# Strassen sevens that finish three of their sums inside PSUM, two products later in the queue

## The chip, the core and the metric

The kernel runs on one core of a Trainium2 chip. The metric is the device time of one execution in microseconds (us): 1163.27 us before the change, the median of three runs (1162.8 to 1163.62). Less is better.

## What is computed

Attention with pooled keys and values makes a matrix x of 2304 tokens by 512. A mixture of four experts follows, and then a gated block whose output is the result:

```python
p = domain_probs / (domain_probs.sum(-1, keepdims=True) + 1e-09)
for e in range(E):                                   # 4 experts
    h = np.maximum(x @ w1[e], 0.0)                   # 512 -> 1024
    out += p[:, e:e + 1] * (h @ w2[e])               # 1024 -> 512
...
a, b = out @ g_w1, out @ g_w2                        # 512 -> 1024 each
result = ((a * b) @ w3) @ w_out
```

Everything is float32. Each matrix product is made from three TensorE matmuls of rounded halves (`mm3`, line 169): high by low, low by high, high by high.

## The kernel before, in words

There are three stretches. Attention and expert 0 take the first 276 us. Then come experts 1 to 3, twelve **hidden batches** (`batch`, line 1176): one for each of four blocks of 576 tokens. At the end, from 882 us on, come eight **gated batches** (lines 1317 to 1430): the four blocks once for each half of the gate columns.

In both kinds of batch the first layer uses Strassen's scheme with seven products in place of eight. `seven(j, sink)` (line 947) handles one pair of 128-column blocks (for a hidden batch, two blocks of the expert's first layer; for a gated batch, one block of each gate), for one block of tokens in two halves of 288. A batch runs four sevens, j = 0 to 3, and then the second layer ("g2"), whose matmuls have 512 columns and which adds up over the four sevens' outputs.

A `product` (line 934) is six matmuls of 128x288 into a PSUM bank. `bank_r` (line 163) deals out the eight banks in turn, and each product of before takes a new one. In the order of the program a seven does this, where u, v and x are scratch tiles, c1 and c0 the two results and every line is one product:

```
x = copy(A11*B11)                  ScalarE (ACT), line 955
  then settle(): what the seven before left over, sink(0)
u = S2*T2 + x                      VectorE (DVE), lines 953, 957
v = S3*T3 + u                      DVE
c1[0] = A22*T4 + v                 DVE
c1[1] = S1*T1 + v; u = S1*T1 + u   DVE, twice; then sink(1)
c0[0] = A12*B21 + x                DVE
c0[1] = S4*B22 + u                 DVE; sink(0) is left for settle()
```

A `sink` passes a result on. The hidden one (line 1160) applies Relu on ACT to all 576 columns, splits the result into halves (ACT copies the high half, line 175; GpSimd, called POOL in the profile, subtracts for the low one, line 176) and copies an edge on POOL. The gated one (line 1308) does nothing for c1, and for c0 multiplies it by c1 on DVE (line 1311) and splits it; `settle()` follows each seven there at once.

The instructions of an engine run in the order of this program; waits between engines follow from the tiles that they read and write. So what stands early in the program on ACT or DVE is done before what stands later, whether or not the later one is ready. Beside the sevens the same engines do other work: `round_some` (weights of later stages, five DVE operations a step, called as `meanwhile` in sevens 1 and 3 of most hidden batches), `stream.split` (ACT and POOL), `weights_of` (line 746: sums and halves of the weights of one pair; ACT, DVE and POOL), `prepare_x` (line 892: sums of the next block of x, called as `next_x` after gated sevens 0 to 2) and `give` (results of the second layer). `fetch_operand` (line 811) brings the operands of the next batch in over the SP queue; the list `USED` (line 809) is their order, and `behind(i)` is the place in the last seven where fetch i is issued.

Of the kernel before, what the change touches and what calls it, by code (L numbers as in the profile page):

```python
# [17 lines left out]
def fused_kernel(  # L18
# [150 lines left out]
    def mm3(ps, lh, ll, rh, rl, first, last):  # L169
        nc.tensor.matmul(ps, lh, rl, start=first, stop=False)  # L170
        nc.tensor.matmul(ps, ll, rh, start=False, stop=False)  # L171
        nc.tensor.matmul(ps, lh, rh, start=False, stop=last)  # L172
# [154 lines left out]
    with tc.manual_schedule():  # L327
# [481 lines left out]
        USED = [B11, T2, T3, T4, T1, B21, B22]  # L809
# [124 lines left out]
        def product(j, a, b):  # L934
            wh, wl = wop_t[j]
            ps = bank_r("s1")[:, :HB]
            for kc in range(2):
                mm3(ps, pick(wh, a, kc), pick(wl, a, kc), operand(kc, 0, b), operand(kc, 1, b), kc == 0, kc == 1)
            return ps
# [7 lines left out]
        def seven(j, sink, meanwhile=None, behind=lambda n: None):  # L947

            x, u, v = (late["small"].tile([P, HB], F32, tag=t, name=t, bufs=1) for t in "xuv")
            c1, c0 = (late["small"].tile([P, 2, HB], F32, tag="c", name=t, bufs=3) for t in ("c1", "c0"))  # L950

            def add(to, one, two):
                nc.vector.tensor_tensor(to, one, two, op=ALU.add)  # L953

            nc.scalar.activation(x, product(j, A11, B11), AF.Copy)  # L955
            settle()
            add(u, product(j, S2, T2), x)
            if meanwhile:
                meanwhile()
            add(v, product(j, S3, T3), u)  # L960
            behind(0)
            add(c1[:, 0], product(j, A22, T4), v)
            behind(1)
            p5 = product(j, S1, T1)
            add(c1[:, 1], p5, v)
            add(u, p5, u)
            sink(1, c1, None)
            behind(2)
            add(c0[:, 0], product(j, A12, B21), x)
            behind(3)  # L970
            add(c0[:, 1], product(j, S4, B22), u)
            pending.append(lambda: sink(0, c0, c1))
# [184 lines left out]
        def hidden(j, b, **kw):  # L1157
            at = (0, P - S % P) if b % 2 else (S - S % P, 0)

            def sink(n, c, other):  # L1160
                fc = j + n * NJ
                t = z_t[fc]
                r = c.rearrange("p a s -> p (a s)")
                nc.scalar.activation(r, r, AF.Relu)  # L1164
                hi_lo(t[:, 0], t[:, 1], r, nc.gpsimd)
                nc.gpsimd.tensor_copy(edge_of(fc)[:, :, at[1]:at[1] + S % P], t[:, :, at[0]:at[0] + S % P])
# [138 lines left out]
        def gated_rows(j):  # L1305
            t = g_t[j]

            def sink(n, c, other):
                if n == 0:
                    r = c.rearrange("p a s -> p (a s)")  # L1310
                    nc.vector.tensor_tensor(r, r, other.rearrange("p a s -> p (a s)"), op=ALU.mult)  # L1311
                    hi_lo(t[:, 0], t[:, 1], r, nc.gpsimd)
            seven(j, sink)
# [3 lines left out]
        for half in range(2):  # L1317
            for n_b, b in enumerate(g_order):
# [11 lines left out]
                if b % 2 == 0:  # L1330
                    edge = late["small"].tile([P, NJ, 2, P], F32R, tag="part", name="edge")
                for j in range(NJ):
                    gated_rows(j)
                    settle()
# [4 lines left out]
                    if b % 2 == 0:  # L1339
                        nc.gpsimd.tensor_copy(edge[:, j, :, :S % P], g_t[j][:, :, S - S % P:])  # L1340
                    else:
                        nc.gpsimd.tensor_copy(edge[:, j, :, P - S % P:], g_t[j][:, :, :P - S % P])
                    if j < 3:
                        next_x(0, spare_slot, j)

# [116 lines left out]
```

## Time and profile before

| what | value |
|---|---|
| time, median of three runs | 1163.27 us |
| span of the profiled execution, first to last instruction | 1162.3 us |
| TensorE (PE) busy | 1150.7 us, 99% |
| weight loads (PEld) busy | 1042.2 us, 90% |
| DVE, POOL, ACT busy | 794.8, 484.9, 382.0 us |
| granted TensorE clock, mean | 1.000 |
| hidden batches 1 to 12 begin | 275.92 to 788.44 us |
| gated batches 1 to 8 begin | 882.04 to 1122.9 us |

The span is the time between the first and the last instruction of one profiled execution; the run's time includes what lies around it. PE's matmuls are pipelined, so their durations overlap: the distance between the starts of two matmuls tells the rate, not the duration of one.

### The profile page before, as it was taken

Reading aid. Unit: us, or ns where it says so; the run is one execution under the profiler, and the core shown is the slowest. Engines: PE = TensorE matmul, PEld = TensorE weight load, DVE = VectorE, ACT = ScalarE, POOL = GpSimd, SP = SyncE. Lnnn points to the kernel's source line nnn. Section 1 sums busy time; section 2 is a strip of 40 time slices with the busy share of each in tenths; the row PEclk is TensorE's granted clock in tenths of the full one; section 3 lists DMA queues with packets and bytes.
Section 4 is the critical chain, followed back from the end, with each engine's and each line's share of the span. In section 5 each row is a group of like instructions: output and inputs, shape, how many; then the busy total and the mean of one; then the engine's idle time right before and its main releaser. Section 6 shows DMA issues by size and latency. Waiting matters only on the chain.

```text
span 1162.3 us, 19412 instructions
## 1 busy us (share of the span) xinstructions
PE 1150.7 (99%) x6806; PEld 1042.2 (90%) x6806; DVE 794.8 (68%) x1624; ACT 382.0 (33%) x699; POOL 484.9 (42%) x563
## 2 busy tenths in 40 slices
PE   7999999999999999999999999999999999999998
PEld 6888898999898998998989989889889999999998
DVE  6867553476586878667678577778687777775454
ACT  4543433245241334421314414124352333231110
POOL 6965212256452647635436745255001222342111
PEclk9999999999999999999999999999999999999999
DMA  9866434554877654668583588686485542945651
GB/s 214 203 151 143 150 104 143 184 195 173 282 235 235 203 149 151 219 191 259 167 264 96 161 237 238 160 267 144 136 192 211 204 166 112 328 162 189 233 189 46
DMA packets 233217, 217.53 MB, mean 187 GB/s; under 512 B 92960, under 2 KB 185376, under 8 KB 233120
## 3 DMA queue, kind: packets, MB, share of 16 engines
q1 hardware_dynamic: 232832, 215.78, 60.4%
q8 instruction: 53, 0.87, 0.3%
q10 hardware_dynamic: 288, 0.52, 0.1%
q14 instruction: 44, 0.36, 0.1%
HBM read 144.41 MB, written 71.83 MB: 186 GB/s over the span
## 4 chain that ended last, share of the span: by engine, by line
PE 93%; DVE 2%; issue 1%; DMA 1%; ACT 1%; POOL 1%; SPq 0%; DVEq 0%; ACTq 0%; POOLq 0%
PE g L171 17%; PE g L172 17%; PE g L170 17%; PE s L170 13%; PE s L171 13%; PE s L172 13%; PE sc L500 1%; PE x_ps L554 1%; PE at_ps L539 1%; DMA plain<-in_k_dram 0%; DMA raw<-in_moe_w_dram 0%; DMA plain<-gate 0%; POOL plain L837 0%; POOL w2l L176 0%; PE vp_ps L448 0%
## 5 line engine op out<-in xcount | busy, mean ns | idle before, releaser
L176 POOL TENSOR_TENSOR round<-plain,round 128x576 fp32r<-128x576 f32 (+1 forms) x131 | 189.7, 1448 | 395.3 <-ACT round L175 324.3
L172 PE MATMUL s<-xo,wh 128*128 128x288 f32 x840 | 248.3, 296 | 0.0
L170 PE MATMUL s<-xo,wh 128*128 128x288 f32 x840 | 248.3, 296 | 0.0
L171 PE MATMUL s<-xo,wl 128*128 128x288 f32 x840 | 247.8, 295 | 0.0
L170 PE MATMUL g<-w2l,round 128*128 128x512 f32 x540 | 211.5, 392 | 0.0
L172 PE MATMUL g<-w2h,round 128*128 128x512 f32 x540 | 210.9, 391 | 0.0
L171 PE MATMUL g<-w2h,round 128*128 128x512 f32 x540 | 210.8, 390 | 0.1
L953 DVE TENSOR_TENSOR plain<-s,plain 128x288 f32<-128x288 f32 x320 | 138.2, 453 | 88.6 <-PE s L172 60.8
L170 PEld LDWEIGHTS s<-xo,wh 128*128 128x128 f32 x840 | 158.0, 188 | 0.7
L171 PEld LDWEIGHTS s<-xo,wl 128*128 128x128 f32 x840 | 157.7, 188 | 0.7
L172 PEld LDWEIGHTS s<-xo,wh 128*128 128x128 f32 x840 | 158.0, 188 | 0.0
L175 ACT ACTIVATE round<-plain 128x576 fp32r<-128x576 f32 (+1 forms) x135 | 90.9, 676 | 162.0 <-DVE plain L1311 158.9
L172 PEld LDWEIGHTS g<-w2h,round 128*128 128x128 f32 x540 | 101.4, 188 | 21.3
L170 PEld LDWEIGHTS g<-w2l,round 128*128 128x128 f32 x540 | 101.5, 188 | 20.5 <-issue 0.8
L171 PEld LDWEIGHTS g<-w2h,round 128*128 128x128 f32 x540 | 101.4, 188 | 20.1 <-DVE round L692 0.4
L955 ACT ACTIVATE plain<-s 128x288 f32<-128x288 f32 x80 | 32.2, 403 | 234.8 <-PE s L172 234.4
L1164 ACT ACTIVATE plain<-plain 128x576 f32<-128x576 f32 x96 | 65.5, 682 | 129.9 <-DVE plain L953 116.9
L288 POOL TENSOR_TENSOR x5l<-x5l 128x256 uint32<-128x256 uint32 x80 | 59.6, 745 | 101.1 <-DVE x5l L287 97.9
L953 DVE TENSOR_TENSOR plain<-s,pb 128x288 f32<-128x288 f32 x160 | 69.6, 456 | 25.7 <-PE s L172 15.2
L692 DVE SCALAR_TENSOR_TENSOR round<-g,round 128x384 fp32r<-128x384 f32 x48 | 26.6, 554 | 69.6 <-ACT round L691 69.4
L170 PE MATMUL g<-xl,round 128*128 128x384 f32 x192 | 66.6, 347 | 0.0
L172 PE MATMUL g<-xh,round 128*128 128x384 f32 x192 | 64.6, 337 | 0.0
(252 smaller groups left out, 2202.3 us busy)
## 6 DMA issues: line engine op xcount, KB each, us to landing
xo<-keptx SPq DMA_DIRECT2D x63, 576.0 KB
raw<-in_moe_w_dram SPq DMA_DIRECT2D x64, 256.0 KB
plain<-acc SPq DMA_DIRECT2D x40, 256.0 KB
keptx<-xo SPq DMA_DIRECT2D x16, 576.0 KB
x5h<-in_moe_w_dram SPq DMA_DIRECT2D x128, 64.0 KB
x5h<-in_moe_w_dram SPq DMA_DIRECT2D x32, 256.0 KB
kept<-xo SPq DMA_DIRECT2D x12, 576.0 KB
acc<-plain SPq DMA_DIRECT2D x26, 256.0 KB
```

The costliest lines, as they stand in the source:

```text
L170: nc.tensor.matmul(ps, lh, rl, start=first, stop=False)
L171: nc.tensor.matmul(ps, ll, rh, start=False, stop=False)
L172: nc.tensor.matmul(ps, lh, rh, start=False, stop=last)
L175: nc.scalar.activation(hi, src, AF.Copy)
L176: (lo_eng or nc.vector).tensor_tensor(lo, src, hi.bitcast(F32), op=ALU.subtract)
L288: nc.gpsimd.tensor_tensor(au, au, bu, op=ALU.add)
L500: nc.tensor.matmul(sc[off:off + n, (hp % 2) * W:(hp % 2 + 1) * W], qT[:, hp, off:off + n], kT_t[b][:, hp * W:(hp + 1) * W], start=True, st ...
L539: nc.tensor.transpose(pt[:NK, g * P:(g + 1) * P], e[:, half * G + g, :], ident)
L692: nc.vector.scalar_tensor_tensor(hl, ps, 0.0, hh.bitcast(F32), op0=ALU.max, op1=ALU.subtract)
L953: nc.vector.tensor_tensor(to, one, two, op=ALU.add)
L955: nc.scalar.activation(x, product(j, A11, B11), AF.Copy)
L1164: nc.scalar.activation(r, r, AF.Relu)
```

## The change

Three additions of each seven go into the matmuls. Where an addend already lies in a PSUM bank, the later product is accumulated onto it (its first matmul has `start=False`): A12*B21 onto the bank of A11*B11, A22*T4 onto the bank of S3*T3 after DVE has added u to that bank in place, and S4*B22 onto the bank of S1*T1 after DVE has added u there. v becomes a copy by ACT. A22*T4, S4*B22 and both sinks of a seven become `rest`, which `settle()` runs after the next seven's second product, or at the end of the batch. A seven takes four banks in place of seven. The sinks read what lies in banks themselves: the hidden one in two Relus of 288 columns, the gated one in two multiplications of 288 and a copy. In gated batches `settle()` moves to the end of the four sevens and the edge copies into the sink. The order of the fetches is changed to fit.

```diff
--- before.py
+++ after.py
@@ -166,10 +166,10 @@
         m = (ring[0] - 1) % 8
         return bank_p(name) if m < 4 else bank_q(m - 4, name)
 
-    def mm3(ps, lh, ll, rh, rl, first, last):
-        nc.tensor.matmul(ps, lh, rl, start=first, stop=False)
-        nc.tensor.matmul(ps, ll, rh, start=False, stop=False)
-        nc.tensor.matmul(ps, lh, rh, start=False, stop=last)
+    def mm3(ps, lh, ll, rh, rl, first, last, onto=False):
+        nc.tensor.matmul(ps, lh, rl, start=first, stop=False, skip_group_check=onto)
+        nc.tensor.matmul(ps, ll, rh, start=False, stop=False, skip_group_check=onto)
+        nc.tensor.matmul(ps, lh, rh, start=False, stop=last, skip_group_check=onto)
 
     def hi_lo(hi, lo, src, lo_eng=None):
         nc.scalar.activation(hi, src, AF.Copy)
@@ -806,7 +806,7 @@
             at = 2 * kc * XO // 4
             return late["xo"][:, at:at + 2 * XO // 4].bitcast(F32)
 
-        USED = [B11, T2, T3, T4, T1, B21, B22]
+        USED = [B11, T2, T3, T1, B21, T4, B22]
 
         def fetch_operand(b, n):
             m = USED[n]
@@ -931,11 +931,12 @@
         def pick(w, a, kc):
             return w[0][:, a, kc] if a < 6 else w[1][:, 0, kc]
 
-        def product(j, a, b):
+        def product(j, a, b, onto=None):
             wh, wl = wop_t[j]
-            ps = bank_r("s1")[:, :HB]
+            ps = bank_r("s1")[:, :HB] if onto is None else onto
             for kc in range(2):
-                mm3(ps, pick(wh, a, kc), pick(wl, a, kc), operand(kc, 0, b), operand(kc, 1, b), kc == 0, kc == 1)
+                mm3(ps, pick(wh, a, kc), pick(wl, a, kc), operand(kc, 0, b), operand(kc, 1, b),
+                    kc == 0 and onto is None, kc == 1, onto is not None)
             return ps
 
         pending = []
@@ -946,30 +947,37 @@
 
         def seven(j, sink, meanwhile=None, behind=lambda n: None):
 
-            x, u, v = (late["small"].tile([P, HB], F32, tag=t, name=t, bufs=1) for t in "xuv")
-            c1, c0 = (late["small"].tile([P, 2, HB], F32, tag="c", name=t, bufs=3) for t in ("c1", "c0"))
-
             def add(to, one, two):
                 nc.vector.tensor_tensor(to, one, two, op=ALU.add)
 
-            nc.scalar.activation(x, product(j, A11, B11), AF.Copy)
+            x, u, v = (late["small"].tile([P, HB], F32, tag=t, name=t, bufs=1) for t in "xuv")
+            p11 = product(j, A11, B11)
+            nc.scalar.activation(x, p11, AF.Copy)
+            p22 = product(j, S2, T2)
             settle()
-            add(u, product(j, S2, T2), x)
+            add(u, p22, x)
+            p21 = product(j, S3, T3)
+            add(p21, p21, u)
+            nc.scalar.activation(v, p21, AF.Copy)
+            p12 = product(j, S1, T1)
+            c1, c0 = (late["small"].tile([P, 2, HB], F32, tag="c", name=t, bufs=3) for t in ("c1", "c0"))
+            add(c1[:, 1], p12, v)
+            add(p12, p12, u)
             if meanwhile:
                 meanwhile()
-            add(v, product(j, S3, T3), u)
             behind(0)
-            add(c1[:, 0], product(j, A22, T4), v)
+            product(j, A12, B21, p11)
             behind(1)
-            p5 = product(j, S1, T1)
-            add(c1[:, 1], p5, v)
-            add(u, p5, u)
-            sink(1, c1, None)
-            behind(2)
-            add(c0[:, 0], product(j, A12, B21), x)
-            behind(3)
-            add(c0[:, 1], product(j, S4, B22), u)
-            pending.append(lambda: sink(0, c0, c1))
+
+            def rest():
+                product(j, A22, T4, p21)
+                behind(2)
+                sink(1, c1, (p21, None), None)
+                product(j, S4, B22, p12)
+                behind(3)
+                sink(0, c0, (p11, p12), c1)
+
+            pending.append(rest)
 
         dec = None
         late["wo"] = rounded(g_wout, "wo")
@@ -1157,11 +1165,12 @@
         def hidden(j, b, **kw):
             at = (0, P - S % P) if b % 2 else (S - S % P, 0)
 
-            def sink(n, c, other):
+            def sink(n, c, banks, *_):
                 fc = j + n * NJ
                 t = z_t[fc]
                 r = c.rearrange("p a s -> p (a s)")
-                nc.scalar.activation(r, r, AF.Relu)
+                for a, bank in enumerate(banks):
+                    nc.scalar.activation(c[:, a], c[:, a] if bank is None else bank, AF.Relu)
                 hi_lo(t[:, 0], t[:, 1], r, nc.gpsimd)
                 nc.gpsimd.tensor_copy(edge_of(fc)[:, :, at[1]:at[1] + S % P], t[:, :, at[0]:at[0] + S % P])
             seven(j, sink, **kw)
@@ -1302,14 +1311,18 @@
         third = [t.rearrange("p a s -> p (a s)").rearrange("p (n s) -> p n s", s=HB) for t in z_t[NJ:]]
         spare_slot = [(third[2 * n][:, :3], third[2 * n + 1]) for n in range(2)]
 
-        def gated_rows(j):
+        def gated_rows(j, at):
             t = g_t[j]
 
-            def sink(n, c, other):
+            def sink(n, c, banks, other):
                 if n == 0:
-                    r = c.rearrange("p a s -> p (a s)")
-                    nc.vector.tensor_tensor(r, r, other.rearrange("p a s -> p (a s)"), op=ALU.mult)
-                    hi_lo(t[:, 0], t[:, 1], r, nc.gpsimd)
+                    for a, bank in enumerate(banks):
+                        nc.vector.tensor_tensor(c[:, a], bank, other[:, a], op=ALU.mult)
+                    hi_lo(t[:, 0], t[:, 1], c.rearrange("p a s -> p (a s)"), nc.gpsimd)
+                    to, p0, s0 = at
+                    nc.gpsimd.tensor_copy(to[:, j, :, p0:p0 + S % P], t[:, :, s0:s0 + S % P])
+                else:
+                    nc.scalar.activation(c[:, 0], banks[0], AF.Copy)
             seven(j, sink)
 
         for kc in range(2):
@@ -1329,19 +1342,16 @@
 
                 if b % 2 == 0:
                     edge = late["small"].tile([P, NJ, 2, P], F32R, tag="part", name="edge")
+                at = (edge, P - S % P, 0) if b % 2 else (edge, 0, S - S % P)
                 for j in range(NJ):
-                    gated_rows(j)
-                    settle()
+                    gated_rows(j, at)
                     if half == 0 and n_b == 0 and j < 2:
                         for f in stores[:4]:
                             f()
                         del stores[:4]
-                    if b % 2 == 0:
-                        nc.gpsimd.tensor_copy(edge[:, j, :, :S % P], g_t[j][:, :, S - S % P:])
-                    else:
-                        nc.gpsimd.tensor_copy(edge[:, j, :, P - S % P:], g_t[j][:, :, :P - S % P])
                     if j < 3:
                         next_x(0, spare_slot, j)
+                settle()
 
                 lead_in = S % P if b % 2 else 0
                 tiles = []
```


## Rows read from the trace of the kernel before

**Rows 1.** The page, parts 1 and 2: busy time by engine; granted TensorE clock in slices

```profile
PE 1150.7 (99%) x6806; PEld 1042.2 (90%) x6806; DVE 794.8 (68%) x1624; ACT 382.0 (33%) x699; POOL 484.9 (42%) x563
...
PEclk9999999999999999999999999999999999999999
```

**Rows 2.** Waits of PE: waiter, releaser: us in total, times, longest us

```profile
PE kT_ps L428 <- POOL pb L420: 4.5, 7, 1.6
...
PE g L171 <- DVE round L176: 0.2, 1, 0.2
```

**Rows 3.** Groups of instructions with shapes kept apart: busy us, mean ns | idle before

```profile
L953 DVE TENSOR_TENSOR plain<-s,plain 128x288 f32<-128x288 f32 x320 | 138.2, 453 | 88.6 <-PE s L172 60.8 <-ACT plain L955 25.4 <-ACT plain L1164 1.6
...
L955 ACT ACTIVATE plain<-s 128x288 f32<-128x288 f32 x80 | 32.2, 403 | 234.8 <-PE s L172 234.4
...
L1164 ACT ACTIVATE plain<-plain 128x576 f32<-128x576 f32 x96 | 65.5, 682 | 129.9 <-DVE plain L953 116.9 <-DMA turned<-plain 9.1 <-DMA plain<-acc 3.8
```

**Rows 4.** Timeline of PE in the first batch's third and fourth seven: start us, us

```profile
287.09 0.30 PE L170 MATMUL s<-xo,wh 128*128 128x288 f32 x1
...
292.67 0.30 PE L170 MATMUL s<-xo,wh 128*128 128x288 f32 x1
...
293.08 0.31 PE L170 MATMUL s<-xo,wh 128*128 128x288 f32 x1
293.23 0.30 PE L171 MATMUL s<-xo,wl 128*128 128x288 f32 x1
```

**Rows 5.** Timeline of ACT beside them

```profile
288.88 0.69 ACT L175 ACTIVATE round<-plain 128x576 fp32r<-128x576 f32 x1
289.47 0.39 ACT L955 ACTIVATE plain<-s 128x288 f32<-128x288 f32 x1
289.76 0.67 ACT L1164 ACTIVATE plain<-plain 128x576 f32<-128x576 f32 x1
290.47 0.69 ACT L175 ACTIVATE round<-plain 128x576 fp32r<-128x576 f32 x1
...
293.70 0.41 ACT L955 ACTIVATE plain<-s 128x288 f32<-128x288 f32 x1 [0.33 <-PE s L172]
```

**Rows 6.** Timeline of DVE there: two additions back to back

```profile
291.05 0.82 DVE L953 TENSOR_TENSOR plain<-s,pb 128x288 f32<-128x288 f32 x2
```

**Rows 7.** Timeline of PE, its weight loads and DVE around one wait of PE

```profile
874.72 0.39 PE L170 MATMUL g<-round 128*128 128x512 f32 x1
...
874.81 0.42 DVE L176 TENSOR_TENSOR round<-raw,round 128x256 fp32r<-128x256 f32 x1
...
875.29 0.19 PEld L171 LDWEIGHTS g<-round 128*128 128x128 f32 x1 [0.61 <-DVE round L176]
...
875.39 0.19 PEld L172 LDWEIGHTS g<-round 128*128 128x128 f32 x1
```

**Rows 8.** Timeline of DVE and ACT in the first batch's second seven

```profile
282.90 0.97 DVE L761 TENSOR_TENSOR plain<-raw 128x256 f32<-128x256 f32 x1 [0.74 <-DMA acc<-plain]
...
285.75 0.39 ACT L955 ACTIVATE plain<-s 128x288 f32<-128x288 f32 x1
```

**Rows 9.** Timeline of PE and DVE in the last batch of the third pass

```profile
788.44 0.29 PE L170 MATMUL s<-xo,wh 128*128 128x288 f32 x1
...
793.61 0.42 DVE L953 TENSOR_TENSOR plain<-s,plain 128x288 f32<-128x288 f32 x1
```

**Rows 10.** Timeline of DVE, PE and ACT between the two passes over the gates

```profile
1007.51 0.76 DVE L1311 TENSOR_TENSOR plain<-plain 128x576 f32<-128x576 f32 x1
1008.19 0.42 DVE L761 TENSOR_TENSOR x5h<-raw 128x256 f32<-128x256 f32 x1
...
1020.44 0.29 PE L170 MATMUL s<-round,wh 128*128 128x288 f32 x1
...
1025.86 0.40 ACT L955 ACTIVATE plain<-s 128x288 f32<-128x288 f32 x1
```

**Rows 11.** Timeline of DVE in the first gated batch: the longest preparation of x

```profile
890.22 1.68 DVE L902 TENSOR_TENSOR x5h<-plain,x5h 128x288 f32<-128x288 f32 x1
```

## Prediction

> **What bounds the kernel.** I read the page's busy times first: TensorE (PE) is busy for 1150.7 of 1162.3 us, at the full granted clock (2.4 GHz) in every slice, while DVE, POOL and ACT stand at 68%, 42% and 33% [rows 1]. Busy matmuls overlap, so this alone doesn't say that PE lacks nothing. The waits of PE are therefore next: of its six kinds the costliest is 4.5 us in all, in attention, and the last is 0.2 us; the wait of a seven for a bank, an operand or an addition is not among them [rows 2]. Third, the timeline of PE: sevens 2 and 3 of the first batch start 5.58 us apart [rows 4], so a product takes 5.58 / 7 = 0.80 us and a matmul 0.133 us. PE is thus the bound, and DVE's additions lie beside it. They can run late without harm: a product takes the next of eight banks, and PE may be some seven products (5.6 us) ahead before it needs a bank back.
>
> **What is removed and added.** There are 20 x 4 = 80 sevens. DVE drops from 7 additions to 4 in each, 240 x 0.453 = 109 us of its busy time [rows 3]. PE's matmuls are the same in number and shape; only the flag of the first one of three products differs, and matmuls with and without that flag are in the row of before at the same rate (the 5.58 us hold both). ACT gains the copy of v, 80 x 0.403 = 32 us, and in each of 96 hidden sinks two Relus of 288 for one of 576, 2 x 0.403 - 0.682 = 0.12 us, 12 us [rows 3]. The gated multiplication in two halves and the copy of c1[0] cost DVE and ACT about an operation more for each of 32 sevens. All this lies on engines with room, under PE's 5.58 us a seven, so it costs nothing where PE need not wait. The POOL copies of the edges are the same ones, issued right behind the same halves, with POOL at 42%. The fetches are as many; each waits on SP for its operand's last product, which for B11 to T1 comes early in the last seven, and for B21, T4 and B22 before the second layer begins. They have that layer to land, and no queue behind them feeds a seven; I cost them at nothing.
>
> **What is new** are waits of PE. In the order of the change A12*B21 may start only when ACT has copied x, A22*T4 when DVE has added u and ACT has copied v, S4*B22 when DVE has added u to S1*T1. PE's queue is in order, so whatever comes next waits too. A bank comes back after eight products or so, as before. The pattern is A11*B11, S2*T2, then A22*T4 and S4*B22 of the seven before, S3*T3, S1*T1, A12*B21. With another seven behind it, v is needed 5 products (4.0 us) after S3*T3 has begun; at the end of a batch the next seven's two and its waiting are missing, and it is 3 products (2.4 us). The cost is where this distance is short, and where ACT or DVE is late already.
>
> **The end of each hidden batch.** Let T be the start of rest(2), two products after the last seven began. PE's own order is A22*T4(2) at T, S4*B22(2) 0.80, S3*T3(3) 1.60, S1*T1(3) 2.39, A12*B21(3) 3.19, A22*T4(3) 3.99. ACT has to do both sinks of seven 2 before v(3). A product's result is in use 1.03 us after its start (292.67 to 293.70) [rows 4, 5]. An ACT operation of 288 lets an independent one begin after 0.29, one of 576 after 0.59, and one that needs it begins 0.03 after its end [rows 5]. So: Relu of c1[0] at T+1.03, of c1[1] 1.32, high half 1.77, Relu 2.36, Relu 2.65, high half 3.09, v at 3.68 until 4.08. DVE's addition to S3*T3 (ready at 2.63 + 0.46 = 3.09) is not the late one. A wait of PE costs the release and a weight load that could not run ahead: 0.06 and 0.10 in the one row that shows it, from the end of DVE's 874.81 + 0.42 to 875.29, and to the next weight load at 875.39 [rows 7]. A22*T4(3) thus starts at 4.24 in place of 3.99, +0.25. DVE's two further additions start at 4.12 and, 0.36 later [rows 6], at 4.48, until 4.94; with 0.16 that is 5.10 against 4.24 + 0.80, another 0.06. Together 0.31 a batch, 12 times: **3.7 us**. Bounds: the release alone and no weight load lost, 0.10, or 1.2 us in all; every ACT operation at its full length (seven of 0.403 or 0.69 and a gap each, v until 4.60) and the second addition behind its first, 0.95, or 11.4 us. An addition written into PSUM isn't in the trace; I take the 0.453 us of one that reads PSUM, and the upper bound has room for 0.1 us more.
>
> **Three places where an engine is late.** First batch, seven 1: ACT's x waits there for `weights_of`, whose sums on DVE start at 282.90 behind a DMA; x runs at 285.75 to 286.14 [rows 8]. In the new order A12*B21(1) would start 11 products after 275.92 (seven 2's 287.09 less two sevens), at 284.69, and gets 286.14 + 0.16: 1.61 late. ACT then still owes seven 0's sinks before v(1): 286.04 and the chain of above to v's end at 289.11, 289.27 against 288.69, 0.58, and 0.06 as above: **2.2 us** (1.5 to 2.6). Last batch of pass three: DVE's queue of weights and second-layer results leaves the first u at 793.61 until 794.03 [rows 9]; addition, v on ACT and release make 795.11 where A22*T4(0) is due 7 products after 788.44, at 794.02: **1.1 us** (0.5 to 1.3). Between the passes over the gates `weights_of` holds DVE and ACT, so that x of the next batch's first seven comes at 1025.86, 5.4 us after its product began [rows 10]. A12*B21(0) is due at 1020.44 + 3.19 = 1023.63 and would wait until 1025.86 + 0.40 + 0.16 = 1026.42, 2.8 us. DVE's chain of weights begins there 0.7 us sooner, since one multiplication of 0.46 replaces an addition and one of 0.76; if all of this reaches x it is 2.0. I take the middle, **2.4 us** (0 if the chain clears by itself, to 2.9).
>
> **Gated batches.** Before v(3) ACT has a copy and one high half only: multiplications at T+1.83, u at 2.20, addition 2.69, v at 3.19 until 3.59, additions at 3.62 and 3.98 until 4.44. Against 3.99 and 4.79, less 0.16 each, this leaves 0.24 and 0.19 us. x's preparation, with a longest operation of 1.68 us on DVE [rows 11], is issued behind the four additions and has until the next seven's multiplications. So **0**, and 0.4 for each of eight (3.2 us) as upper bound.
>
> **Sum.** 3.7 + 2.2 + 1.1 + 2.4 = 9.4 us. The span of 1162.3 us becomes 1171.7; the runs' median lies 1.0 us above the span, which I leave: **1172.7 us**. The bounds add up to 3.2 (1166.5) and 21.4 us (1184.7).
>
> **Against the change** speaks that three of a seven's four banks now stay open while other engines read and write them. By rows 4 to 6 the products between hide this, but for the last seven of a batch. If nothing hid it, each seven would show an addition, the copy of v and two additions, 0.46 + 0.40 + 0.36 + 0.46 = 1.7 us, and 80 of them 134 us; this is rival 5. The Trainium skill, "Perfetto Trace Analysis", section "Matmuls", has a rule on this side: independent groups of matmuls should go round different PSUM banks, so that emptying one overlaps the next group's matmuls.
>
> **Rivals.** (1) *The waits are covered*, and the time is that of before, 1163.3 us, not slower. Its place is ACT's order: if v(3) ends by T+3.83 in place of 4.08, and with 240 additions gone the late x and u come before 1023.5, 284.5 and 794, PE never waits. For it: DVE's 109 us; against: x is late there by `weights_of` and DMA, not by additions. 11%. (2) *ACT's chain is longer*, no overlap of its operations or dearer PSUM access: 11.4 us for 3.7, and up to 3.2 in the gated batches, 1180 to 1184 us. For it: the chain has seven operations in a row; against: rows 5 show the overlap. 17%. (3) *Faster*: PE's matmuls are up to 0.15 us apart in places (293.08 to 293.23) [rows 4], against a mean of 0.133; if engines reading PSUM cause that and the change relieves them by 0.1 us a seven, 8 us go, 1155 us. Against: reads of PSUM become more, not fewer. 5%. (4) *The clock*: after its first instruction PE stood still for at most 1.6 us at a time (longest wait of the first row) [rows 2] and kept its full clock [rows 1]; a stop of 2.4 us is new. Were the clock to fall to 1.2 GHz for one batch's four sevens, 22.3 us would be added, 1195 us. 3%. The Trainium skill, "TensorE: Matmul & The Clock Gate", section "What's actually happening", has an idle engine fall back to that level; no row of this trace shows it. (5) *Open banks stop PE in every seven*: 1163.3 + 134 = 1297 us. Against: DVE and ACT need 1.7 us of the 4.0 us that they have. 1%.
>
> **How the numbers follow.** My forecast, waits at batch ends and the three late places, gets 63%: 1166.5 to 1178 us. About 0.2% (2.3 us) is what a measurement of this kernel can tell from no change. Forecast, it and rivals 2, 4 and 5 are slower by more than that, 84%; rival 1 is the same, 11%; rival 3 is faster, 5%. The range takes part of rival 1 and most of rival 2 in: 1164 to 1181 us.
>
> **What would show it.** Waits of PE, or gaps between matmuls, for ACT's copies and DVE's additions at s: one of some 0.3 us before the last product but one of each hidden batch's sevens, three larger ones near 286, 795 and 1024 us. Within the sevens 0.80 us a product, as before. If the batches' sevens still take 22.3 us each, rival 1 or 3 holds; if the gaps stand in every seven, rival 5 does; if they stand at the ends but at 0.6 us and more, rival 2.

## The result, and the profile after

The change makes the kernel slower: 1173.05 us, the median of four runs (1171.64 to 1173.96), against 1163.12 us of before (also four). The ratio is 1.0083, its 95% interval 1.0069 to 1.0097. The span of the profiled execution, the slowest of the four, is 1172.2 us, 9.9 us more than before. The page's busy times, which answer to [rows 1]:

```profile
PE 1156.9 (99%) x6806; PEld 1043.5 (89%) x6806; DVE 692.0 (59%) x1416; ACT 432.1 (37%) x907; POOL 477.9 (41%) x563
```

DVE has lost 103 us of work and ACT has gained 50, and nothing of the 103 has come off the span. That is what PE at 99% meant in [rows 1]: DVE's work lay beside PE's. The groups with shapes kept apart (busy us, mean ns, idle before), as in [rows 3], say what the new operations cost:

```profile
L951 DVE TENSOR_TENSOR s<-s,plain 128x288 f32<-128x288 f32 x160 | 73.7, 461 | 58.3 <-PE s L172 54.7 <-DVE plain L951 0.5
...
L961 ACT ACTIVATE pb<-s 128x288 f32<-128x288 f32 x80 | 32.2, 403 | 42.9 <-DVE s L951 42.9
```

The addition in place, PSUM to PSUM, takes 461 ns, 8 ns more than one from PSUM to SBUF; the copy of v takes the 403 ns of the copy of x. So no new operation is dear. What is new are waits. Of the views of PE's waits (waiter, releaser: us in all, times, longest), first that of the matmuls, as in [rows 2]:

```profile
PE s L170 <- ACT plain L955: 3.0, 2, 2.3
...
PE s L170 <- ACT pb L961: 0.6, 2, 0.3
```

and that of the weight loads, which go ahead of the matmuls and so meet most waits first:

```profile
PEld s L170 <- ACT pb L961: 4.8, 14, 0.6
PEld s L170 <- ACT plain L955: 3.5, 2, 2.5
```

L961 is the copy of v, awaited 14 times (12 batch ends and two late places); L955 is the copy of x, awaited twice. The length of each batch's four sevens, from its first matmul's start to the start of the matmul that follows its last one, shows where the 9.9 us are:

| batches | before, us | after, us | difference, us |
|---|---|---|---|
| ten hidden ones | 22.34 each | 22.69 each | 10 x 0.35 = 3.5 |
| first hidden one (275.20) | 22.34 | 24.47 | 2.13 |
| last of pass three (793.63) | 22.34 | 23.40 | 1.06 |
| first of the second gate pass (1026.51) | 22.40 | 26.26 | 3.86 |
| seven other gated ones | 22.28 to 22.35 | 22.28 to 22.33 | 0.0 |
| all twenty | 446.72 | 457.29 | 10.6 |

The span grew by 0.7 less, since the first batch begins at 275.20, not at 275.92. That is scatter: in the profiles of the change, A, B, B2, F and G, whose programs are the same up to there, it begins between 274.32 and 276.33. Within the sevens the rate is nearly what it was (0.132 us a matmul, 0.133 before).

The end of a hidden batch, in the second one, as PE, ACT and DVE show it in the timeline (start us, us). T, the start of A22\*T4 of the third seven, is 338.14:

```profile
338.14 0.29 PE L170 MATMUL s<-xo,wh 128*128 128x288 f32 x1
...
339.20 0.41 ACT L1173 ACTIVATE plain<-s 128x288 f32<-128x288 f32 x1 [1.23 <-PE s L172]
...
339.51 0.44 ACT L1173 ACTIVATE plain<-plain 128x288 f32<-128x288 f32 x1
...
339.98 0.69 ACT L175 ACTIVATE round<-plain 128x576 fp32r<-128x576 f32 x1
...
340.57 0.69 ACT L1173 ACTIVATE plain<-s 128x288 f32<-128x288 f32 x2
...
341.29 0.69 ACT L175 ACTIVATE round<-plain 128x576 fp32r<-128x576 f32 x1
...
341.88 0.39 ACT L961 ACTIVATE pb<-s 128x288 f32<-128x288 f32 x1
341.96 0.29 PE L172 MATMUL s<-xo,wh 128*128 128x288 f32 x1
342.33 0.19 PEld L170 LDWEIGHTS s<-xo,wh 128*128 128x128 f32 x1 [0.31 <-ACT pb L961]
342.33 0.40 PE L170 MATMUL s<-xo,wh 128*128 128x288 f32 x1
...
342.57 0.30 PE L171 MATMUL s<-xo,wl 128*128 128x288 f32 x1
...
342.74 0.46 DVE L951 TENSOR_TENSOR s<-s,plain 128x288 f32<-128x288 f32 x1
```

ACT runs seven operations without a pause, v last, and v ends at 342.27. PE's matmul starts 0.06 us later, at 342.33, where it was due at 342.09; the matmul behind it comes after 0.24 us in place of 0.13, since its weights (342.44 in the trace) could not be loaded ahead. DVE's second addition ends at 343.20 and S4\*B22 starts at 343.25, 0.02 late, and again 0.24 passes behind its first matmul.

The dearest place is the stop between the two passes over the gates. PE's timeline there (with the wait that it shows), and ACT's copy of x:

```profile
1029.58 0.29 PE L172 MATMUL s<-xo,wh 128*128 128x288 f32 x1
...
1031.68 0.40 ACT L955 ACTIVATE plain<-s 128x288 f32<-128x288 f32 x1
...
1032.13 0.61 PE L170 MATMUL s<-round,wh 128*128 128x288 f32 x1 [2.26 <-ACT plain L955]
1032.54 0.44 PE L171 MATMUL s<-round,wl 128*128 128x288 f32 x1
1032.78 0.44 PE L172 MATMUL s<-round,wh 128*128 128x288 f32 x1
```

After the stop the matmuls come 0.24 us apart, until 1035.2. The view by windows (length, busy us of PE, PEld, DVE, ACT, POOL, then granted clock, DMA share, GB/s) has the reason:

```profile
1026.00:1029.50 3.50, 3.50 (x26) 3.38 (x26) 3.47 (x5) 2.99 (x7) 2.53 (x2) 1.00 0.54 203
1029.50:1032.00 2.50, 0.38 (x3) 0.14 (x2) 1.88 (x4) 1.85 (x4) 1.27 (x2) 0.96 0.16 61
1032.00:1035.20 3.20, 3.07 (x13) 3.07 (x14) 1.75 (x4) 0.49 (x2) 1.75 (x2) 0.50 0.84 235
1035.20:1040.00 4.80, 4.80 (x38) 4.80 (x38) 1.92 (x5) 1.92 (x4) 0.94 (x1) 1.00 0.82 330
```

The granted clock is 0.50 for these 3.2 us, which is 1.2 GHz, and PE looks busy there (3.07 of 3.20) while it does half the work.

### The profile page after: what moved, and what is told of

It reads as the page before. It is cut to its first block, busy times and chain, and to the rows that moved or that the text cites. A ratio compares the mean times of both kernels' runs of the same rounds, so it can differ in the third digit from the quotient of the medians.

```text
span 1172.2 us, 19164 instructions
## 1 busy us (share of the span) xinstructions
PE 1156.9 (99%) x6806; PEld 1043.5 (89%) x6806; DVE 692.0 (59%) x1416; ACT 432.1 (37%) x907; POOL 477.9 (41%) x563
## 4 chain that ended last, share of the span: by engine, by line
PE 87%; ACT 5%; DVE 3%; DMA 2%; issue 2%; POOL 1%; SPq 0%; ACTq 0%; DVEq 0%; POOLq 0%
PE g L171 16%; PE g L172 16%; PE g L170 16%; PE s L170 12%; PE s L172 11%; PE s L171 11%; ACT round L175 2%; ACT plain L1173 1%; PE sc L500 1%; PE at_ps L539 1%; PE x_ps L554 1%; DMA raw<-in_moe_w_dram 1%; DMA x5h<-in_moe_w_dram 0%; DMA plain<-in_k_dram 0%; ACT pb L961 0%
## 5 line engine op out<-in xcount | busy, mean ns | idle before, releaser
L955 ACT ACTIVATE plain<-s 128x288 f32<-128x288 f32 x80 | 32.9, 411 | 296.9 <-PE s L172 296.8
L951 DVE TENSOR_TENSOR s<-s,plain 128x288 f32<-128x288 f32 x160 | 73.7, 461 | 58.3 <-PE s L172 54.7
L951 DVE TENSOR_TENSOR plain<-s,pb 128x288 f32<-128x288 f32 x80 | 36.6, 457 | 68.8 <-ACT pb L961 63.7
L1173 ACT ACTIVATE plain<-s 128x288 f32<-128x288 f32 x144 | 53.0, 402 | 57.1 <-PE s L172 53.7
L951 DVE TENSOR_TENSOR plain<-s,plain 128x288 f32<-128x288 f32 x80 | 36.2, 453 | 61.2 <-PE s L172 55.5
```

Of the source, the lines that this page charges most:

```text
L955: nc.scalar.activation(x, p11, AF.Copy)
L1173: nc.scalar.activation(c[:, a], c[:, a] if bank is None else bank, AF.Relu)
```

## The experiments

The theory was: accumulating is free for PE; the late places of two products are free too; the loss is in short waits where A22\*T4, S4\*B22 and A12\*B21 now depend on ACT's and DVE's copies and additions. Its rivals: the late places or the changed fetches cost the time (D decides); accumulating onto a bank that others have read and written is slow by itself (A and E); waits of other kinds. Runs A, B, D and F share one chip and runs of before with a median of 1163.74 us (14 runs); the others share one with 1163.94 us (15 runs).

### D: the late places alone

No product accumulates; DVE makes all seven additions again, and the two products, the sinks and the fetches stay in their new places.

```diff
-            add(p21, p21, u)
-            nc.scalar.activation(v, p21, AF.Copy)
+            add(v, p21, u)
...
-            product(j, A12, B21, p11)
+            add(c0[:, 0], product(j, A12, B21), x)
...
-                product(j, A22, T4, p21)
+                add(c1[:, 0], product(j, A22, T4), v)
...
```

> No accumulation: seven banks a seven and all additions on DVE as before the change, but A22*T4, S4*B22 and the sinks stay in their late places (after the next seven's second product). Theory 1: the late places alone cost nothing, since no product waits for DVE or ACT but by the bank it takes, eight products back: 1162.5 to 1164 us, each hidden batch's sevens 22.3 us long without gaps. Rival (the late products are the cost, as they end later and hold the second layer up): 1167 us and more.

Measured: 1162.42 us (1161.88 to 1163.14, ten runs), ratio 0.9989 (0.9979 to 0.9998). All sevens take 22.21 to 22.26 us a batch without a gap, but for the batch at 786.99 with 23.22; there the sevens wait twice (spacings of 0.40 and 0.69 us), for results of `give` (line 1243). The view of PE's waits has one of the two:

```profile
PE s L170 <- DVE pb L1243: 0.4, 1, 0.4
```

The late places and the new order of fetches thus cost nothing; the whole loss belongs to the accumulations and what feeds them.

### E: the accumulations in the old places

The other half alone: A22\*T4, S4\*B22 and A12\*B21 accumulate as in the change, but stand where the kernel before had them, within their own seven.

```diff
             add(p21, p21, u)
             nc.scalar.activation(v, p21, AF.Copy)
...
+            product(j, A22, T4, p21)
+            p12 = product(j, S1, T1)
...
+            sink(1, c1, (p21, None), None)
+            product(j, A12, B21, p11)
+            product(j, S4, B22, p12)
             def rest():
-                product(j, A22, T4, p21)
...
                 sink(0, c0, (p11, p12), c1)
```

> The accumulations without the late places: A22*T4 directly behind S3*T3, S4*B22 two products behind S1*T1, as the products stood before the change; the sink of c1 at once. Theory 1: each seven now shows what the late places hide: A22*T4 waits for the addition and the copy of v, 1.3 us, S4*B22 for DVE's two additions, 0.4 us: 80 x 1.7 = 135 us more, less what the late x and u cost the changed kernel (it is hidden in these waits): 1290 to 1310 us. If accumulating itself were the cost and not the waits, the place would not matter: 1173 us.

Measured: 1316.62 us (two runs), ratio 1.1309 (1.1288 to 1.133), a little above what was expected. The waits of the weight loads are now there in every one of the 80 sevens:

```profile
PEld s L170 <- ACT pb L961: 106.7, 80, 4.8
PEld s L170 <- DVE s L951: 37.7, 78, 0.8
```

The timeline of PE has a matmul that waited for the copy of v and one that waited for an addition in place, each with the matmul before it:

```profile
402.01 0.29 PE L172 MATMUL s<-xo,wh 128*128 128x288 f32 x1
403.30 0.40 PE L170 MATMUL s<-xo,wh 128*128 128x288 f32 x1 [1.00 <-ACT pb L961]
...
405.65 0.29 PE L172 MATMUL s<-xo,wh 128*128 128x288 f32 x1
406.18 0.40 PE L170 MATMUL s<-xo,wx 128*128 128x288 f32 x1 [0.23 <-DVE s L951]
```

Before A22\*T4 1.3 us pass between matmuls, before S4\*B22 some 0.5, and 0.24 behind each, where 0.13 is the rate: 1.17 + 0.37 + 2 x 0.11 = 1.76 us a seven. That is the price that the late places hide: 80 x 1.76 = 141 us of the 152.7 lost, and most of the rest stands at the three late places. So the two halves of the change belong together: one costs nothing and the other is ruinous without it.

### A: the copy of v on DVE

```diff
-            nc.scalar.activation(v, p21, AF.Copy)
+            nc.vector.tensor_copy(v, p21)
```

> v is copied out of the bank by DVE, right behind the addition, and no longer by ACT behind both sinks of the seven before; all else as in the changed kernel (1173.05 us). Theory 1 (the waits at the end of hidden batches are for ACT's queue): v ends at about T+3.55 in place of T+4.1, so the gaps before the last two products of the twelve hidden batches (0.35 us a batch net, 4.2 us) go, and of the first batch's second wait about 0.5 us; the wait of 3.9 us between the passes over the gates stays: 1168 to 1169 us. Theory 2 (accumulating onto a bank that another engine has written is itself dear for TensorE): the gaps stay, 1172.5 to 1174 us.

Measured: 1167.9 us (1166.79 to 1168.72, five runs), ratio 1.0033 (1.002 to 1.0046). The timeline of the second batch has v and ACT's high half side by side, where ACT did one after the other:

```profile
339.99 0.46 DVE L961 COPY pb<-s 128x288 f32<-128x288 f32 x1
340.07 0.69 ACT L175 ACTIVATE round<-plain 128x576 fp32r<-128x576 f32 x1
```

The hidden batches, except the first and the last, take 22.22 us without a gap, though three products of each seven still accumulate onto banks that DVE has written. So accumulating is free for PE, and the end of a hidden batch costs what ACT's queue makes it cost. The gated batches gain nothing (22.32 to 22.37 us): there the spacing behind S4\*B22's first matmul is 0.24 us, as DVE's second addition, now behind the copy, ends only 0.06 us before that matmul. The three late places stay: 23.33 us for the first batch (it keeps the wait for x and loses that for v), 23.46 for the last of pass three, 24.94 for the stop between the gate passes.

### F: v copied twice on ACT

The copy of v is issued twice in a row on ACT, to see whether its time reaches PE.

```diff
             nc.scalar.activation(v, p21, AF.Copy)
+            nc.scalar.activation(v, p21, AF.Copy)
```

> The suspected cost doubled: ACT copies v twice in a row, so v is final about 0.30 us later and nothing else changes. Theory 1: every hidden batch's end waits 0.30 us longer, 3.6 us; the gated ends, where I worked out 0.2 us of slack, wait some 0.1 us longer, 0.7 us; the places where ACT is late (first batch, last batch of pass three) 0.3 us each: 1177 to 1178.5 us, and no gap elsewhere, since 1.4 us and more are free there. Theory 2 (ACT's queue is not what ends the waits): 1173 us.

Measured: 1182.76 us (1182.2 to 1183.45, four runs), ratio 1.0162 (1.0147 to 1.0177): the right places, but dearer than expected. The timeline at the end of the second batch:

```profile
342.02 0.39 ACT L961 ACTIVATE pb<-s 128x288 f32<-128x288 f32 x1
342.44 0.41 ACT L962 ACTIVATE pb<-s 128x288 f32<-128x288 f32 x1
...
342.90 0.40 PE L170 MATMUL s<-xo,wh 128*128 128x288 f32 x1 [0.52 <-ACT pb L962]
```

The second copy starts 0.42 us after the first, not 0.3, as it writes the same tile. So each hidden batch grows by 0.43 us (22.69 to 23.12), and most gated ones by 0.44 (22.32 to 22.75), where v's slack is used up and A22\*T4 comes some 0.3 us late, with the lost weight load behind it. The three late places grow too (25.50, 24.65 and 26.83 us). Within all other sevens there is no gap, so ACT's time counts only where the distance is short.

### B and B2: A12\*B21 in a bank of its own

A12\*B21 goes to a bank of its own and DVE adds x, so that PE no longer waits for x. In B the addition stands where the product was, behind the rounding step (`meanwhile`):

```diff
             if meanwhile:
                 meanwhile()
             behind(0)
-            product(j, A12, B21, p11)
+            add(c0[:, 0], product(j, A12, B21), x)
...
-                sink(0, c0, (p11, p12), c1)
+                sink(0, c0, (None, p12), c1)
```

> A12*B21 goes into a bank of its own again and DVE adds x (one of the three accumulations undone; the other two and the late places stay). Theory 1: the long wait between the passes over the gates is A12*B21 waiting for ACT's late x; it moves to A22*T4 of the same seven, which is due 2.4 us later, and shrinks from 2.4 to about 1.6 us; with the shorter stop TensorE's clock should not fall, which gives back another 1.2 us. In the first batch the wait only moves from A12*B21 to A22*T4. Ends of batches unchanged. 1170.5 to 1171.5 us. Theory 2 (accumulating itself is dear): a third of it goes, wherever the accumulations stand, some 3 us spread over all batches, 1170 us, with smaller gaps at batch ends.

Measured: 1179.85 us (1178.75 to 1181.34, four runs), ratio 1.0136 (1.0118 to 1.0154): a miss by 8 us. The place it was made for did what was expected (the batch after the gate passes takes 24.05 us with a stop of 1.69). But most hidden batches with rounding steps take 23.3 to 23.9 us, with gaps of 0.2 to 0.4 us before A22\*T4(2) and 0.7 before A22\*T4(3). DVE and ACT in the timeline of the second batch show why:

```profile
334.35 0.29 DVE L287 TENSOR_SCALAR x5l<-x5h 128x256 f32<-128x256 uint32 x1
334.56 0.45 DVE L951 TENSOR_TENSOR plain<-s,plain 128x288 f32<-128x288 f32 x1
335.10 0.41 ACT L955 ACTIVATE plain<-s 128x288 f32<-128x288 f32 x1 [3.51 <-DVE plain L951]
335.41 0.41 ACT L1173 ACTIVATE plain<-s 128x288 f32<-128x288 f32 x1
```

x is one tile. The new addition reads x(1) only behind the five operations of the rounding step (L282 to L287), so ACT can't write x(2) before 335.10, and the sinks and v, which stand behind x(2) in ACT's queue, are late with it. B2 tests that reading: the product and its addition are put ahead of the rounding step.

```diff
+            add(c0[:, 0], product(j, A12, B21), x)
             if meanwhile:
                 meanwhile()
             behind(0)
-            add(c0[:, 0], product(j, A12, B21), x)
```

> As the kernel with A12*B21 in a bank of its own, but this product and its addition of x stand ahead of the rounding step on DVE and not behind it. My reading of that kernel's 1179.9 us: x is one scratch tile, the addition of x behind the rounding step of sevens 1 and 3 keeps the next seven's copy of x from starting, and this copy is first in ACT's queue, ahead of both sinks and of v. If so, the gaps in sevens 2 and the 0.7 us gaps at batch ends fall back to none and 0.4 us, and the time is what I had expected there: 1170.5 to 1171.8 us. If the bank of its own (or the fifth bank a seven takes) is the cause: 1179 us and more.

Measured: 1172.34 us (1171.1 to 1176.03, four runs), ratio 1.0074 (1.0056 to 1.0092), half a microsecond above the upper end of what was expected. The batches are as they should be: 22.72 us for the hidden ones, no gap before A22\*T4(2), 24.08 for the one after the gate passes. The same two operations, in B2's timeline:

```profile
333.28 0.45 DVE L951 TENSOR_TENSOR plain<-s,plain 128x288 f32<-128x288 f32 x1
...
333.82 0.41 ACT L955 ACTIVATE plain<-s 128x288 f32<-128x288 f32 x1 [1.31 <-DVE plain L951]
```

B2's second batch begins at 322.72 and B's at 321.81, so counted from there the addition comes 2.19 us sooner (10.56 us after the batch began, not 12.75) and x(2) with it. So B's loss was its place in DVE's queue. Its ratio is still not far from the change's 1.0083: the stop between the gate passes is the only place that gains (2.2 us), while the ends of the hidden batches (0.38 us each) and the first batch (24.61 us) stay as dear.

### G: useless products in the long stop

Three products S1\*T1, 18 matmuls, go into a bank that nobody reads, ahead of A12\*B21 in the first seven after the gate passes. They take the time of the stop and do no useful work; if the low clock follows from the stop, it should vanish.

```diff
+            for _ in range(fill):
+                product(j, S1, T1)
             product(j, A12, B21, p11)
...
-                    gated_rows(j, at)
+                    gated_rows(j, at, 3 if half == 1 and n_b == 0 and j == 0 else 0)
```

> In the first seven after the change of gates (the one where TensorE stands still for 2.4 us) three copies of the product S1*T1 (18 matmuls, 2.4 us) are issued ahead of A12*B21 into a bank that nobody reads: TensorE works on something useless where it waited. Theory 1a (after the stop the granted clock is 0.50, and 12 or more matmuls start 0.24 in place of 0.133 us apart): A12*B21 begins at the same time, but at full clock; 1.2 to 1.5 us go wherever the changed kernel's run had a clock under 1.000: 1171.5 to 1172 us in every run, mean clock 1.000. Rival (the slow matmuls after the stop are slow because of what the other engines and the transfers do then): the 0.24 us spacing stays, 1173 us.

Measured: 1172.6 us (1171.59 to 1172.97, five runs), ratio 1.007 (1.0057 to 1.0082). The windows that showed the stop and the low clock in the change's profile:

```profile
1029.50:1032.00 2.50, 2.50 (x21) 2.50 (x20) 2.35 (x5) 1.39 (x3) 1.25 (x2) 1.00 0.36 135
1032.00:1035.20 3.20, 3.20 (x25) 3.08 (x24) 1.76 (x4) 1.36 (x4) 2.24 (x2) 1.00 0.62 179
```

The clock is 1.00 throughout, the matmuls are 0.13 us apart right behind the place of the stop (but for one 0.24), and the batch takes 24.83 us, 1.4 less than 26.26. That the filled stop is what kept the clock up is not shown: A's kernel has the same stop unfilled, its one profile has a clock of 1.00 behind it too (rows in the last section), and its batch takes 24.94 us. What A and G show is the size: some 1.3 of the 1.4 us are the clock's, and 0.1 is the weight load lost behind a wait, which A's batch pays as well. The median is only 0.5 us below the change's, above the 1171.5 to 1172 us that were expected, and the intervals of the two ratios overlap. In the same profile the last batch of pass three lost 0.7 us more than in the change's (24.09 against 23.40), because DVE reached the first u 5.29 us after that batch began, and not 4.61, though both programs are the same up to there; scatter of this size hides what G looked for.

### H: D with its rounding steps moved

D's waits stood at results of `give` in the last batch of pass three. H is D with other numbers of rounding steps in the second layers of an expert's first three batches: 7, 8 and 6 in place of 6, 8 and 7.

```diff
-                some = 8 if n == 1 else 6 + n // 2
+                some = 8 if n == 1 else 7 - n // 2
```

> The late places without accumulation (1162.4 us in the run of before), with one rounding step moved from the third block's batch of each expert to the first block's (7, 8 and 6 steps for 6, 8 and 7). There the only waits left were 1.0 us in the last batch of pass three, for DVE's second-layer results behind its rounding steps. If these are what ends the wait, it goes: 1161 to 1161.8 us, below the kernel before the change. If the transfers that the steps wait for are the limit, the wait stays or moves: 1162.4 us.

Measured: 1161.72 us (1160.31 to 1163.2, eleven runs), ratio 0.9981 (0.9973 to 0.999). That is the lowest of all, and under the kernel before by a margin at the edge of what can be told. It is not shown to be better than D: the intervals of the two ratios overlap, and in H's profile (of its slowest run) the wait at 788 us is gone (22.22 us for that batch), but a spacing of 1.47 us, for a result of `give` again, stands in the second batch, so that the twenty batches' sevens take 445.9 us against D's 445.4. The wait has moved, as the other of the two expected cases has it.

## Why the prediction was right, and where its sum was not

The forecast was 1172.7 us and the measurement 1173.05; the span was to grow by 9.4 and grew by 9.9. The steps:

- **PE bounds, DVE's cover is free.** Right: 103 us of DVE removed bring nothing in the span (109 for the additions alone were forecast), and the rate within the sevens stays. ACT's copy of v takes 32.2 us as worked out, its two Relus 74.0 in place of 65.5 (8.5 more, 12 forecast), and all that stays under PE.
- **Ends of hidden batches**, 0.31 us each forecast, 0.35 measured. ACT's chain was nearly exact: v starts at T+3.74 (3.68 forecast) and ends at T+4.13 (4.08). A22\*T4(3) loses 0.24 to the wait and 0.11 to the weight load behind it, S4\*B22(3) loses 0.02 and 0.11; the forecast charged the lost weight load to the wait once and found it partly hidden the second time. 0.48 in all is cut to 0.35 because the 168 matmuls run 0.12 us quicker in the new order, which A and D show without any wait (22.22 against 22.34). A confirms the cause, and F that v's own time is what counts.
- **First batch**, 2.2 forecast, 1.78 besides its end. x comes late and PE waits twice, as said; but x ends 9.68 us after the batch began, where before's row gives 10.22 [rows 8]. The half microsecond is one operation of DVE, the first sum of weights: 0.97 us long in the trace of before, where a subtraction of POOL runs beside it, and 0.42 in the change's, where none does. The two lines are from the timelines of before (POOL) and of the change (DVE):

```profile
282.15 1.43 POOL L176 TENSOR_TENSOR round<-plain,round 128x576 fp32r<-128x576 f32 x1 [2.21 <-DVE plain L953]
282.12 0.42 DVE L761 TENSOR_TENSOR plain<-raw 128x256 f32<-128x256 f32 x1 [2.32 <-DMA acc<-plain]
```

  In both traces the operation waits for a DMA and starts 6.9 to 7.0 us after the batch began. D and H, with all seven additions on DVE, have it at 0.42 to 0.43 us too, and x at 9.92 and 9.63. In E, with the old places, the third sum runs beside POOL's subtraction and takes 1.65 us. So by these traces the late places moved POOL's work away; the shorter queue of DVE, rival 1's argument, isn't what brought it.
- **Last batch of pass three**, 1.1 forecast, 0.71 besides its end: u starts 4.61 us after the batch began, 5.17 before [rows 9]. In G, the same program up to there, it starts at 5.29, and the batch loses 0.7 us more; the timelines of DVE, first the change's, then G's, whose batches begin at 793.63 and 793.36:

```profile
798.24 0.42 DVE L951 TENSOR_TENSOR plain<-s,plain 128x288 f32<-128x288 f32 x1
798.65 0.42 DVE L951 TENSOR_TENSOR plain<-s,plain 128x288 f32<-128x288 f32 x1
```

  So the difference to the forecast is no more than the scatter between executions, and that fewer additions on DVE made u earlier isn't shown.
- **Between the gate passes**, 2.4 forecast, 3.86 measured: this is the term that was mis-sized. The stop itself is exactly as forecast: A12\*B21(0) was due at 1029.71 and started at 1032.13, 2.42 us late. x starts 5.17 us after the batch began, before 5.42 [rows 10], so only 0.25 of the 0.7 us reached it, while PE started 0.05 behind x and not 0.16. What was not in the sum is the restart at 1.2 GHz: twelve spacings, 3.05 us in all from 1032.13 to 1035.18, against 12 x 0.132 = 1.58, so 1.47 us, of which 0.11 is the lost weight load that A's matmul behind the same stop pays at full clock. The forecast named this as rival 4, at 3% and with four sevens (22.3 us) as its size; it came in this profile, and at a fifteenth of that size. The Trainium skill, "TensorE: Matmul & The Clock Gate", section "What's actually happening", has the idle engine fall back to 1.2 GHz; the row of granted clock 0.50 now agrees, and A's row of 1.00 behind an equal stop says that it need not come.
- **Gated batches**, 0 forecast and 0.0 measured, but by two things that cancel. v ends 0.18 to 0.23 us before A22\*T4(3) starts, where the forecast had 0.40 (3.59 against 3.99); since a matmul follows its releaser by 0.05, that is still enough, and F's second copy uses it up. DVE's second addition ends 0.06 to 0.10 before S4\*B22(3), where the forecast had 0.35: its first matmul is in time, but the weight load behind it is late, so that 0.20 to 0.23 us pass. The timeline of PE at the end of the first gated batch:

```profile
909.55 0.29 PE L172 MATMUL s<-xo,wh 128*128 128x288 f32 x1
909.68 0.39 PE L170 MATMUL s<-xo,round 128*128 128x288 f32 x1
909.91 0.29 PE L171 MATMUL s<-xo,round 128*128 128x288 f32 x1
```

  That 0.1 us a batch stands against what the new order gains: D's gated batches take 22.21 to 22.26 us, the change's 22.28 to 22.33.
- **Rival 5**, open banks that stop PE in every seven, was priced at 1.7 us a seven; E shows 1.76 where the late places are taken away. The Trainium skill, "Perfetto Trace Analysis", section "Matmuls", wants independent groups to go round different banks; E, where three products take the bank of an earlier one, agrees, with its 1.76 us a seven, and the change beside E shows that a distance of several products takes nearly all of that away with the same banks.

The errors are small and of both signs: 12 x 0.04 = 0.5 for the ends, -0.4 and -0.4 for two late places, 1.5 for the restart, -0.7 for the earlier start of the first batch, together 0.5 us. That they come so near to nothing is luck: the restart at the low clock, the early u and the early first batch belong to this execution. The forecast also left out what the new order gives back. Against D's sevens, which have that order and no accumulation (444.4 us without D's own 1.0 of waits), the accumulations cost 12.9 us, and the order takes 2.3 of it off.

What stays open: where the 0.12 us a batch of the new order comes from, and why DVE reaches the late places sooner in one execution than in another. Neither was tried by itself. A version that accumulates where there is slack and adds on DVE at the last seven of each batch wasn't tried either; by D and A it should come near D, but hardly below it, since PE bounds both.

## What to carry to other kernels

Taking work off an engine that lies beside the bound brought nothing here (103 us of DVE); ask first which waits the new form gives to the engine that bounds. A matmul that accumulates onto a bank which other engines edit makes PE wait for them, and here that was free where other products enough stood between (from S3\*T3 to A22\*T4 it is five products in the middle of a hidden batch, and at its end three, too few while v stands behind both sinks in ACT's queue); look at the ends of the loops, where there are fewer, and at each place where an engine's queue is already late. And what is issued first in a queue decides: B with an addition behind a rounding step stood at 1.0136, B2 with the same addition ahead of it at 1.0074.

## What the runs showed that was not expected

- A stop of 2.55 us between two matmuls was followed by 3.2 us at a granted clock of 0.50 in the change's profile. In A's the same stop, of the same 2.55 us at the same place, was followed by full clock at once:

```profile
1023.60:1026.20 2.60, 0.34 (x4) 0.10 (x2) 1.87 (x5) 1.94 (x4) 1.36 (x2) 1.00 0.13 46
1026.20:1029.40 3.20, 3.20 (x24) 3.20 (x25) 2.15 (x5) 0.41 (x1) 1.58 (x2) 1.00 0.82 239
```

  In F's profile, after 2.56 us, the clock fell only after a few matmuls at full rate (0.58 in the mean of 1039.4 to 1043.4); in E's a gap of 2.2 us was enough at one place, while one of 2.7 us in its first batch was followed by 1.00. So a stop of this length may cost its own time alone or some 1.3 us more, and one profile doesn't tell which a run will have.
- A matmul that PE had to hold was followed at full clock by a spacing of 0.20 to 0.24 us, up to 0.11 above the rate, whatever it waited for (ACT's copy, DVE's addition, a result of `give`): this is a second price of even the shortest wait, and the ends of the gated batches pay it without any delay of the held matmul itself.
- The new order moved the sevens by 0.12 us in 22.34, though each batch has the same 168 matmuls of the same shapes. D and A both show it, with seven banks a seven and with four, so the number of banks isn't what brings it.
